# Where weights are decoded in the first slots of a fused top-k attention and feed-forward kernel

## The chip, the cores and the metric

The kernel runs on one core of a Trainium2 chip. The metric is the device time of one launch in microseconds. The engines are named as the profile names them: PE is TensorE's matmuls, PEld its weight loads, DVE is VectorE, ACT is ScalarE, POOL is GpSimd, and SP is the queue that issues most transfers.

## The reference

An attention that keeps, for each query, the 32 largest scores, and then a feed-forward that multiplies a hidden value by its own cosine.

```python
scores = scale * np.matmul(q, k.transpose(0, 1, 3, 2))      # 8 batches, 8 heads, 576 x 576, head size 64
kth = np.partition(scores, -top_k, axis=-1)[..., -top_k:-top_k + 1]
scores = np.where(scores >= kth, scores, -1000000000.0)
attn = np.exp(scores - np.max(scores, axis=-1, keepdims=True))
attn = attn / (np.sum(attn, axis=-1, keepdims=True) + 1e-09)
o = np.matmul(attn, v)
x = o.transpose(0, 2, 1, 3).reshape(4608, 512)
h = x @ w_in                                                  # 512 x 2048
out = (h * np.cos(h)) @ w_out                                 # 2048 x 512
```

q, k and v are single precision; w_in and w_out come in double precision, and the kernel turns them into single precision itself.

## The kernel before

**Units and slots.** The work is cut into 144 units: 36 blocks of 128 tokens by 4 pairs of heads. The main loop (L820) runs one slot for each unit. In slot i VectorE finds the 32 largest of each row of unit i, in four rounds of max and replace over two folded halves of the scores (`rest`, the larger of each pair, and `low`, the smaller). The same slot also ends the softmax of unit i-1 (`w`), sends the probabilities of unit i-2 (`x`) through memory to transpose them, and on even slots multiplies the probabilities of units i-4 and i-3 (`z`) with v. The scores of later units are made up to two slots ahead.

**Within a slot** (`slot`, L711) everything is issued by hand in one order, and each engine works through its own part of that order without overtaking. On VectorE: fold (L247), rounds 0 to 2 (L352 max, L357 replace), the shifts of the weights (L144), round 3 with the search of `low`, inside it the products that make xT (L486), then the sum and the reciprocal of the softmax (den L399, L404). On ScalarE: weight loads issued, sine (L592), mask (L381, L383), banks emptied (L551, L553, L622), exponentials (L391, with a table load after a sine), the copies of the next scores (L236, L237), and the first step of the weights' decoding (L133, L136). On GpSimd: the split of the probabilities into 16-bit halves (L424, L426), the making of `low` (L265, L274), the adds of the weights (L154), the reductions of the sine's argument (L573, L582), the gate g * cos (L599).

**`low` on two engines.** For units in `BUSY` (L95, 7 to 11) VectorE makes `low` itself with one more instruction (`fold_now`, L255). For the others GpSimd does it with an add and a subtraction (`fold_sum`, `fold_low`).

**Weights.** There are 32 chunks of 128 x 512, 16 of w_in and 16 of w_out. `load_weights` (L103) loads a number of them in each slot: in the first two slots on SP's queue, then on ScalarE's. A chunk is then decoded in three steps in a later slot: ScalarE (`decode_first`, at the end of the slot in which it was loaded), one shift on VectorE (`decode_second`) and one add on GpSimd (`decode_third`) in the next slot. `decode_third` takes the chunks last in, first out. Loaded chunks lie in seven buffers that the feed-forward's g also uses.

**Feed-forward.** `feed` (L646) is called three times in a slot and issues steps by credit: a step A b.i of the first product (`ff1`, block b, i from 0 to 7, 8 matmuls of 128 x 128) or a step B b.j of the second (`ff2`, two matmuls of 128 x 512). Two A steps fill one bank, which ScalarE empties (`take_banks`); after two banks GpSimd reduces the argument, ScalarE takes the sine, and GpSimd gates. `ff["kind"]` and `ff["half"]` hold which kind is next and whether one step of it has been done. A step is issued only when its weights have been decoded in an earlier slot and its gate lies two calls back; otherwise the other kind is taken. From the middle of the run a pair of slots holds 4 A steps, 4 B steps, the scores of 2 units and P@V of 2.

**P@V.** `values(z)` (L462 onwards, matmuls at L477) writes to a part of the bank `rim`, which also holds the ends of the scores. `take_values` (L481) makes xT of it, the input of the A steps: A b.0 needs xT of all four units of block b.

**Loads of the first slots.** `at_once` (L694 to L697) issues on SP's queue: v of head pair hp in slot hp, and q and k of pairs 2 and 3 in slots 0 and 1. Later loads have slots of their own (`at_slot`).

Of the kernel before, what the change touches and what calls it, by code (L numbers as in the profile page):

```python
# [30 lines left out]
def kernel(  # L31
# [16 lines left out]
    NP = H // 2  # L48
# [35 lines left out]
    for i in range(DF // CW):  # L84
        w = consts.tile([P, NC, CW], F32, tag=f"w_in{i}", name=f"w_in{i}")
# [4 lines left out]
    for f in range(NF):  # L90
        w = consts.tile([P, DM], F32, tag=f"w_out{f}", name=f"w_out{f}")
        w_out.append(w)
        chunks.append((moe_w_out[f * P : (f + 1) * P, :], w))
    CHUNKS, XB = 7, 4
    BUSY = range(7, 12)  # L95
    ff = {"live": 0, "tick": 0, "now": 0, "credit": 0.0, "end": False, "kind": 0, "half": 0, "open": 0, "late": False}

    wq = {"next": 0, "loaded": deque(), "second": deque(), "third": deque(), "done": 0, "ready": 0}
# [40 lines left out]
    def decode_second(n):  # L139

        for _ in range(min(n, len(wq["second"]))):
            st, w, spare = wq["second"].popleft()
            wi = w.bitcast(I32)
            nc.vector.tensor_scalar(  # L144
                out=wi, in0=wi, scalar1=3, scalar2=None, op0=ALU.logical_shift_left
            )
            wq["third"].append((st, w, spare))

    def decode_third():

        while wq["third"]:
            st, w, _ = wq["third"].pop()
            wi = w.bitcast(I32)
            nc.gpsimd.tensor_tensor(out=wi, in0=wi, in1=st[:, :, 0], op=ALU.add)  # L154
            wq["done"] += 1
# [5 lines left out]
    units = []  # L161
    for t0 in range(0, B * S, P):
        parts = []
        for i, a in enumerate((t0, t0 + TAIL)):
            b, q0 = a // S, a % S
# [75 lines left out]
    def fold_high(u):  # L241

        s, sc = u["s"], u["sc"]
        if u["n"] not in BUSY:
            del u["sc"]
# [5 lines left out]
    def fold_now(u):  # L251

        s, sc = u["s"], u.pop("sc")
        u["low"] = work.tile([P, 2, HS], F32, tag="low", name="low", bufs=1)
        nc.vector.tensor_tensor(  # L255
            out=u["low"], in0=sc[:, :, 0:HS], in1=s[:, :, HS:S], op=ALU.min
        )

    def fold_sum(u):

        if not u["folds"]:
            return
        s = u["s"].bitcast(I32)
        u["low"] = work.tile([P, 2, HS], F32, tag="low", name="low", bufs=1)
        nc.gpsimd.tensor_tensor(  # L265
            out=u["low"].bitcast(I32), in0=s[:, :, 0:HS], in1=s[:, :, HS:S], op=ALU.add
        )

    def fold_low(u):

        if not u["folds"] or u["n"] in BUSY:
            return
        low = u["low"].bitcast(I32)
        nc.gpsimd.tensor_tensor(  # L274
            out=low, in0=low, in1=u["rest"][:, :, HS:S].bitcast(I32), op=ALU.subtract
        )
# [15 lines left out]
    def topk_first(u, w):  # L292
# [5 lines left out]
        if u["folds"]:  # L298
            if u["n"] not in BUSY:
                fold_sum(u)  # L300
# [3 lines left out]
        if merges:  # L304
            merge_second(w)
        if u["folds"] and u["n"] in BUSY:
            fold_now(u)
        topk_round(u, 0, [lambda: bounds(w), lambda: distances(w)] if w else ())

    def topk_round(u, rnd, between=(), ahead=None):  # L310
        top, rest, lasts = u["top"], u["rest"], TOPK // 8 - 1
        end = TOPK - 1 - 8 * rnd
        at = top[:, :, end : end - 8 if rnd < lasts else None : -1, 0]
        if u["folds"]:
            search(
                at, rest[:, :, HS:S] if rnd == 0 else rest[:, :, 0:HS], rest[:, :, 0:HS], rnd < lasts,
                between if rnd < lasts else (),
            )
        else:
            search(at, u["s"] if rnd == 0 else rest, rest, rnd < lasts, between)  # L320
        if rnd < lasts:
            return
        del u["rest"]
        if u["folds"]:
            low = u.pop("low")
            for k in range(TOPK // 16):
                more = k < TOPK // 16 - 1
                if ahead and not more:
                    take_values(ahead)
                search(  # L330
                    top[:, :, 1 + 8 * k : 9 + 8 * k, 1], low, low, more,
                    () if more or rnd < lasts else between,
                )
# [10 lines left out]
    def merge_second(u):  # L344
        nc.vector.tensor_reduce(
            out=u["top"][:, :, TOPK - 1, 1], in_=u.pop("lesser"), axis=mybir.AxisListType.X,
            op=ALU.max,
        )

    def search(to, src, rest, more, between=()):  # L350
        for j in range(2):
            nc.vector.max(to[:, j], src[:, j])  # L352
            if between:
                between[j]()
        if more:
            for j in range(2):
                nc.vector.match_replace(rest[:, j], to[:, j], src[:, j], NEG)  # L357
# [39 lines left out]
    def sums(u):  # L397
        den = small.tile([P, 2], F32, tag="den", name="den")
        nc.vector.tensor_reduce(out=den, in_=u["den"], axis=mybir.AxisListType.X, op=ALU.add)  # L399
        u["den"] = den  # L400

    def reciprocal(u):
        u["rden"] = small.tile([P, 2], F32, tag="rden", name="rden")
        nc.vector.reciprocal(u["rden"], u.pop("den"))  # L404

    def both(u):
        return [lambda: sums(u), lambda: reciprocal(u)] if u else ()
# [71 lines left out]
    def take_values(us):  # L479
        blk, hp, n = block_of[us[0]["tok"]], us[0]["hp"], len(us)  # L480
        if "xT" not in blk:  # L481
            blk["xT"] = work.tile([P, NP, P], F32, tag="xT", name="xT", bufs=5)
        for i, u in enumerate(us):
            to, o, pT = blk["xT"][:, hp + i], room[0][:, i * P : (i + 1) * P], u.pop("pT")
            if u["paired"]:
                nc.vector.tensor_tensor(out=to, in0=o, in1=pT[:, 2 * NT + 1], op=ALU.mult)  # L486
            else:
                nc.scalar.copy(out=to, in_=o)
        blk["left"] -= n
        blk["tick"] = ff["tick"]  # L490
# [15 lines left out]
    first = deque((blk, i) for blk in blocks for i in range(2 * NF * blk["w"] // 512))  # L506
# [165 lines left out]
    LAST = NU - NP  # L672
# [7 lines left out]
    at_slot, at_once = {}, {}  # L680
# [7 lines left out]
    for n in range(NP, len(order)):  # L688
        i = last[order[n - 5]] if n >= 5 else 0
        load_at(max(i, 2 * NP + 2), load_qk, *order[n])  # L690
        i = last_values[order[n - 6]] if n >= 6 else 0
        load_at(max(i + 4 - i % 2, 2 * NP + 2), load_v, *order[n])

    for hp in range(NP):  # L694
        at_once[hp] = [(load_v, 0, hp)]
    for hp in range(2, NP):
        at_once[hp - 2].append((load_qk, 0, hp))  # L697

# [6 lines left out]
    def send(x):  # L705

        split(x)
        write_halves(x)
        transposes(x)

    def slot(i, u, w, x, z):  # L711
        n = (3, 4, 3, 2)[i] if i < NP else 2 if i < 2 * NP else 3
        if i < NP:
            for load, b, hp in at_once[i]:
                load(b, hp)
        load_weights(n, nc.sync if i < 2 else nc.scalar)
        if x:
            send(x)
        decoding = i < 3 * NP
        ff["late"] = False  # L720
        topk_first(u, w)
        fold_low(u)
        topk_round(u, 1)
        topk_round(u, 2)
        if decoding:
            sines(1)
            gate(1)
        decode_second(NP)
        decode_third()
        reduce_first()  # L730
        reduce_second()
        made = scored.get(i, [])
        if z:
            take_banks()
        feed(1)

        for m in made:
            scores(m)
        if z:
            values(z)  # L740


        late = len(made) > 0

        if i % 2 and not decoding:
            sines(1)
        if w:
            mask(w)
        take_banks()
        if w and late:  # L750
            exponentials(w)
        take_scores(units[i + 1])
        if w and not late:
            exponentials(w)
        topk_round(u, 3, both(w), z)
        ff["late"] = not decoding
        if i in at_slot:
            load, b, hp = at_slot[i]
            load(b, hp)
        gate(1)  # L760
        feed(1 if len(made) == 2 else 2)
        take_banks()
        decode_first(NP)
        reduce_first()
        reduce_second()
        feed(1 if len(made) == 2 else 3)
        if i == LAST:
            sines(1)
# [51 lines left out]
    for i in range(NU + 1):  # L820
        ff["end"] = i >= NU
        ff["credit"] = min(ff["credit"] + 5.0 - 0.9 * len(scored.get(i, [])), 5.3)
        ff["now"] += 1
        wq["ready"] = wq["done"]
        u, w = (units[i - n] if 0 <= i - n < NU else None for n in range(2))
        x = units[i - 2] if 0 <= i - 2 < LAST else None
        z = units[i - 4 : i - 2] if i % 2 == 0 and 0 <= i - 4 < LAST else None
        if i <= LAST:
            slot(i, u, w, x, z)
        else:  # L830
            last_slot(i, u, w, x, z)
# [47 lines left out]
```

## Time and profile before

| | |
|---|---|
| median of three runs (lowest, highest) | 1460.69 us (1459.52, 1464.77) |
| profiled execution: device time, span | 1461.65 us, 1459.9 us |
| busy share of the span: PE, PEld, DVE, ACT, POOL | 95%, 68%, 93%, 75%, 79% |
| span by the chain that ended last: PE, DVE, ACT, DMA | 82%, 8%, 4%, 3% |
| sum of A steps on PE (L537) and of B steps (L612) | 540.1 us, 538.1 us |
| sum of max (L352) and replace (L357) on DVE, four groups | 1221.3 us |
| the weights' decoding on POOL: the mean of one add (L154) | about 1.26 us |

Shares of busy time are means over the whole span. The page's picture of the span in 40 slices, each 36.5 us long, shows the start and the end apart:

```profile
PE   4387899999999999999999999999999999999998
DVE  7999999999999999999999999999999999999821
PEclk6598999999999999999999999999999999999999
DMA  8986687666665576657655666657665566655300
```

Each digit is the busy share of one slice in tenths. The first four slices or so are a start in which there is little feed-forward yet and the DMA engines are full; then PE and DVE are both full; in the last two slices the attention is done and only the feed-forward of the last blocks is left.

Slots can be found in the trace by L247, the first large instruction of a slot on DVE: slot 0 starts at 7.28 us, slot 1 at 17.83, slot 7 at 81.57, slot 8 at 91.86, slot 9 at 103.92, slot 10 at 114.55, slot 11 at 127.48, slot 12 at 138.11, slot 13 at 147.98, slot 14 at 158.81.

### The profile page before, as it was taken

What the parts mean: (1) busy time and instruction counts of PE and PEld (TensorE: products, weight loads), DVE (VectorE), ACT (ScalarE), POOL (GpSimd) and SP (SyncE); (2) the same over time, 40 slices, a digit from 0 to 9 for tenths busy, and PEclk for the clock granted to TensorE, in tenths of its full rate; (3) what the DMA queues carried; (4) which work ended last, traced back from release to release, by engine and by line L of the source; (5) the groups of instructions that cost most, each with busy time, mean ns of one, the idle gap of its engine ahead of it and who ended that gap; (6) DMA issues with size and microseconds to landing.
All of it is one profiled execution on the core that took longest, in us unless ns stands there. A gap on an engine that the chain in (4) does not pass through costs nothing.

```text
span 1459.9 us, 30230 instructions
## 1 busy us (share of the span) xinstructions
PE 1386.9 (95%) x10288; PEld 996.8 (68%) x10288; DVE 1363.8 (93%) x5213; ACT 1088.2 (75%) x1910; POOL 1157.5 (79%) x812
## 2 busy tenths in 40 slices
PE   4387899999999999999999999999999999999998
PEld 2265667777777767777777776777777777777665
DVE  7999999999999999999999999999999999999821
ACT  5787767877777777778777777777777787877641
POOL 5867878888888888888888887888888888888410
PEclk6598999999999999999999999999999999999999
DMA  8986687666665576657655666657665566655300
GB/s 254 282 235 192 175 183 182 155 161 190 179 159 152 168 180 169 161 144 201 185 168 143 144 180 182 170 149 185 192 169 144 152 171 168 166 152 152 62 8 15
DMA packets 427434, 240.00 MB, mean 164 GB/s; under 512 B 375952, under 2 KB 392592, under 8 KB 427280
## 3 DMA queue, kind: packets, MB, share of 16 engines
q1 hardware_dynamic: 418704, 216.88, 57.0%
q10 hardware_dynamic: 8576, 21.19, 4.1%
q8 instruction: 81, 1.33, 0.4%
q14 instruction: 73, 0.60, 0.1%
HBM read 45.09 MB, written 101.19 MB: 100 GB/s over the span
## 4 chain that ended last, share of the span: by engine, by line
PE 82%; DVE 8%; ACT 4%; DMA 3%; POOL 1%; issue 1%; SPq 1%; ACTq 0%; POOLq 0%
PE mm L537 31%; PE o L612 31%; PE rim L477 10%; PE sc L226 7%; DVE top L352 4%; DVE rest L357 2%; PE rim L226 2%; DMA v<-in_v_dram 1%; ACT s L391 1%; ACT s L383 1%; DMA k<-in_k_dram 1%; ACT L391 1%; DMA st<-in_moe_w_in_dram 1%; DVE rest L247 1%; DVE low L357 0%
## 5 line engine op out<-in xcount | busy, mean ns | idle before, releaser
L537 PEld LDWEIGHTS mm<-xT,w_in 128*128 128x128 f32 x4608 | 537.0, 192 | 74.8 <-issue 64.7
L612 PE MATMUL o<-w_out,g 128*128 128x512 f32 x1152 | 538.1, 600 | 12.0 <-POOL w_out L154 7.7
L537 PE MATMUL mm<-xT,w_in 128*128 128x128 f32 x4608 | 540.1, 275 | 6.8 <-ACT x L553 3.9
L352 DVE MAX8 top<-rest 128x8 f32<-128x288 f32 x1148 | 480.7, 454 | 0.0
L424 POOL COPY halves<-s 128x2304 uint16<-128x2304 uint16 x140 | 294.8, 2105 | 149.5 <-ACT s L391 149.1
L357 DVE MATCH_REPLACE8 rest<-top,rest 128x288 f32<-128x288 f32 (+1 forms) x860 | 377.0, 446 | 0.0
L612 PEld LDWEIGHTS o<-w_out,g 128*128 128x128 f32 x1152 | 202.4, 190 | 199.0 <-issue 184.2
L352 DVE MAX8 top<-low 128x8 f32<-128x288 f32 x568 | 240.0, 448 | 0.1
L391 ACT ACTIVATE s<-s,nd 128x576 f32<-128x576 f32 x288 | 220.2, 767 | 0.8
L383 ACT ACTIVATE s<-s,top 128x576 f32<-128x576 f32 x288 | 206.1, 766 | 0.0
L274 POOL TENSOR_TENSOR low<-low,rest 128x576 int32<-128x576 int32 x137 | 193.6, 1413 | 10.7
L265 POOL TENSOR_TENSOR low<-s 128x576 int32<-128x576 int32 x137 | 193.7, 1414 | 6.1 <-ACT s L237 4.9
L226 PE MATMUL sc<-k,q 64*128 64x448 f32 (+1 forms) x640 | 157.9, 591 | 36.8 <-DMA k<-in_k_dram 14.9
L551 ACT ACTIVATE g<-mm 128x512 f32<-128x512 f32 x144 | 85.8, 596 | 128.8 <-PE mm L537 124.6
L582 POOL TENSOR_TENSOR x<-g,x 128x1024 f32<-128x1024 f32 x68 | 160.9, 2366 | 5.7
L477 PE MATMUL rim<-pT,v 128*64 128x128 f32 (+1 forms) x2560 | 159.5, 269 | 2.8 <-DMA pT<-rows 2.8
L599 POOL TENSOR_TENSOR g<-g,x 128x1024 f32<-128x1024 f32 x68 | 161.0, 2367 | 1.3 <-ACT x L592 1.3
L477 PEld LDWEIGHTS rim<-pT,v 128*64 128x64 f32 x2560 | 132.8, 139 | 13.1 <-issue 4.0
L236 ACT COPY s<-sc 128x896 f32<-128x896 f32 x144 | 129.2, 897 | 3.9 <-PE sc L226 3.4
L237 ACT COPY s<-rim 128x256 f32<-128x256 f32 x144 | 55.1, 382 | 91.9 <-PE rim L477 91.9
L357 DVE MATCH_REPLACE8 low<-top,low 128x288 f32<-128x288 f32 x284 | 123.6, 443 | 0.0
L226 PEld LDWEIGHTS sc<-k,q 64*128 64x128 f32 (+1 forms) x640 | 47.5, 183 | 100.2 <-DVE rest L357 47.0
(59 smaller groups left out, 1335.8 us busy)
## 6 DMA issues: line engine op xcount, KB each, us to landing
rows<-halves SPq DMA_DIRECT2D x140, 640.0 KB, 3.0
out_dram<-ob ACTq DMA_DIRECT2D x36, 256.0 KB, 2.4
q<-in_q_dram SPq DMA_DIRECT2D x31, 288.0 KB, 3.9
v<-in_v_dram SPq DMA_DIRECT2D x32, 256.0 KB, 3.4
st<-in_moe_w_out_dram ACTq DMA_DIRECT2D x16, 512.0 KB, 5.1
st<-in_moe_w_in_dram SPq DMA_DIRECT2D x10, 512.0 KB, 6.9
k<-in_k_dram SPq DMA_DIRECT2D x31, 144.0 KB, 3.8
k<-in_k_dram SPq DMA_DIRECT2D x32, 128.0 KB, 3.8
```

What stands on the lines that cost most here:

```text
L226: nc.tensor.matmul(to[r0 : r0 + rows, j, 0 : k1 - k0], st["q"][d, q0 : q0 + rows], st["k"][d, k0:k1], start=True, stop=True,)
L265: nc.gpsimd.tensor_tensor(out=u["low"].bitcast(I32), in0=s[:, :, 0:HS], in1=s[:, :, HS:S], op=ALU.add)
L274: nc.gpsimd.tensor_tensor(out=low, in0=low, in1=u["rest"][:, :, HS:S].bitcast(I32), op=ALU.subtract)
L352: nc.vector.max(to[:, j], src[:, j])
L357: nc.vector.match_replace(rest[:, j], to[:, j], src[:, j], NEG)
L383: nc.scalar.activation(out=s[:, j], in_=s[:, j], func=AF.Prelu, bias=less[:, j, 1:2], scale=1.0, alpha=FAR)
L391: nc.scalar.activation(out=s[:, j], in_=s[:, j], func=AF.Exp, bias=nd[:, j : j + 1], scale=SCALE, accum_out=den[:, j, 0:1],)
L424: nc.gpsimd.tensor_copy(out=halves[:, :, 0 : 2 * S], in_=s.rearrange("p (k h) -> p h k", h=2))
L477: nc.tensor.matmul(o[d, to], lhsT, rhs, start=c == 0, stop=c == NT)
L537: nc.tensor.matmul(mm[:, at : at + w], w_in[f // FC][:, c, (f % FC) * P : (f % FC + 1) * P], blk["xT"][:, c], start=c == 0, stop=c == NC - 1,)
L599: eng.tensor_tensor(out=g, in0=g, in1=x, op=ALU.mult)
L612: nc.tensor.matmul(o, g[:, at : at + P], w_out[f], start=f == 0, stop=f == NF - 1)
```

## The change

There are six edits.

- `BUSY` begins at unit 8: `low` of unit 7 is made on GpSimd.
- The numbers of chunks loaded in each slot are 3, 3, 3, 2, 2, 2, 3, 3, 3, 3, then 2, instead of 3, 4, 3, 2, 2, 2, 2, 2, then 3.
- From slot 7 on (`early` false) the shifts and adds of the weights stand after round 3 instead of after round 2, and the adds take the chunks first in, first out.
- v of pair 3 is loaded in slot 2, together with v of pair 2, instead of in slot 3.
- P@V of units 0 and 1 is made in slot 5 instead of slot 4; units 2 and 3 follow in slot 6 as before.
- On even slots from 12 on, the kind of the next feed-forward step is set: the second half of an open bank of A if there is one, else B.

```diff
-    BUSY = range(7, 12)
+    BUSY = range(8, 12)
...
-    def decode_third():
+    def decode_third(early):
 
         while wq["third"]:
-            st, w, _ = wq["third"].pop()
+            st, w, _ = wq["third"].pop() if early else wq["third"].popleft()
...
     for hp in range(NP):
-        at_once[hp] = [(load_v, 0, hp)]
+        at_once.setdefault(min(hp, 2), []).append((load_v, 0, hp))
...
     def slot(i, u, w, x, z):
-        n = (3, 4, 3, 2)[i] if i < NP else 2 if i < 2 * NP else 3
+        n = (3, 3, 3, 2, 2, 2, 3, 3, 3, 3)[i] if i < 10 else 2
+        early = i < 2 * NP - 1
+        if i % 2 == 0 and i >= 3 * NP:
+            ff["kind"], ff["half"] = (0, 1) if first and first[0][1] % 2 else (1, 0)
         if i < NP:
-            for load, b, hp in at_once[i]:
+            for load, b, hp in at_once.get(i, ()):
                 load(b, hp)
...
-        decode_second(NP)
-        decode_third()
+        if early:
+            decode_second(NP)
+            decode_third(early)
         reduce_first()
         reduce_second()
...
         topk_round(u, 3, both(w), z)
+        if not early:
+            decode_second(NP)
+            decode_third(early)
         ff["late"] = not decoding
...
-        z = units[i - 4 : i - 2] if i % 2 == 0 and 0 <= i - 4 < LAST else None
+        z = units[i - 4 : i - 2] if i % 2 == 0 and NP < i < LAST + 4 else None
+        if i == NP + 1:
+            z = units[0:2]
```

The order in which instructions are issued changes up to slot 12 and is the same from slot 13 to the end. In slots 7 to 12 the changed kernel has shifts of 3, 3, 2, 3, 2 and 1 chunks, where the kernel before has 2, 2, 3, 2, 3 and 1. The adds of slots 7, 9 and 11 stand ahead of the reductions and of the next slot's split on GpSimd. In slot 12 the step A 1.5 is issued ahead of the scores, where it stood after P@V.

## The prediction

> **What bounds the kernel now.** I read the table of windows first, one row per stretch, with each engine's busy time, the granted TensorE clock and the DMA share.
>
> ```profile
> 25.00:50.00 25.00, 7.93 (x24) 3.54 (x24) 23.42 (x87) 21.57 (x43) 21.66 (x18) 0.50 0.96 282
> 100.00:125.00 25.00, 17.34 (x91) 9.80 (x90) 24.93 (x84) 20.84 (x39) 18.07 (x13) 0.80 0.67 211
> 150.00:175.00 25.00, 21.57 (x155) 14.86 (x154) 23.36 (x91) 20.22 (x35) 22.81 (x16) 1.00 0.56 167
> 300.00:400.00 100.00, 100.00 (x720) 72.73 (x719) 98.93 (x388) 78.86 (x136) 86.99 (x61) 1.00 0.68 184
> 1350.00:1400.00 50.00, 45.95 (x354) 33.67 (x353) 39.49 (x115) 33.34 (x65) 22.96 (x19) 1.00 0.23 47
> ```
>
> From 175 to 1350 us TensorE (first column after the length) has no gap worth naming. Before 150 us it idles and VectorE (third) is full. So there are two regimes, and I looked for the seam in the timeline of TensorE:
>
> ```profile
> 115.26 2.08 PE L612 MATMUL o<-w_out,g 128*128 128x512 f32 x2 [7.66 <-POOL w_out L154]
> ...
> 156.83 1.98 PE L612 MATMUL o<-w_out,g 128*128 128x512 f32 x4 [2.16 <-POOL g L599]
> ...
> 167.08 3.39 PE L537 MATMUL mm<-xT,w_in 128*128 128x128 f32 x28 [1.27 <-DVE xT L486]
> ```
>
> The last gap ends at 167.08, where the first feed-forward matmul of block 2 waits for VectorE's xT of slot 14 (issued at 166.75). Everything after is TensorE work in a fixed order, 1292.8 us to the end of the span. The orders of issue of the two kernels agree on every engine from slot 13 on, and by the end of slot 12 both have issued the same feed-forward work. So the end moves by what slot 14's xT moves, and only slots 1 to 13 count.
>
> In those slots VectorE is the clock. Its timeline (start, length, operation, idle before) shows the stalls, two of them inside the shift's own duration:
>
> ```profile
> 61.85 0.75 DVE L247 TENSOR_TENSOR rest<-sc,s 128x576 f32<-128x576 f32 x1
> 71.51 0.75 DVE L247 TENSOR_TENSOR rest<-sc,s 128x576 f32<-128x576 f32 x1
> 81.57 0.75 DVE L247 TENSOR_TENSOR rest<-sc,s 128x576 f32<-128x576 f32 x1
> 87.85 0.75 DVE L144 TENSOR_SCALAR w_out<-w_out 128x512 int32<-128x512 int32 x2
> 98.14 1.97 DVE L144 TENSOR_SCALAR w_out<-w_out 128x512 int32<-128x512 int32 x2
> 120.83 3.00 DVE L144 TENSOR_SCALAR w_out<-w_out 128x512 int32<-128x512 int32 x2
> 158.11 0.16 DVE L399 TENSOR_REDUCE den<-dens 128x2 f32<-128x4 f32 x1 [1.56 <-ACT s L391]
> ```
>
> Two shifts cost 0.75 us alone but 1.97 and 3.00 here. GpSimd's timeline says why, and also shows the chain from the adds to the gate in slots 7 and 8:
>
> ```profile
> 88.73 2.57 POOL L154 TENSOR_TENSOR w_out<-w_out,st 128x512 int32<-128x512 int32 x2 [5.75 <-ACT s L391]
> 91.26 1.07 POOL L573 TENSOR_SCALAR x<-x 128x1024 f32<-128x1024 int32 x1
> 92.41 2.36 POOL L582 TENSOR_TENSOR x<-g,x 128x1024 f32<-128x1024 f32 x1
> 94.72 2.10 POOL L424 COPY halves<-s 128x2304 uint16<-128x2304 uint16 x1
> 97.12 2.37 POOL L599 TENSOR_TENSOR g<-g,x 128x1024 f32<-128x1024 f32 x1
> ...
> 121.01 2.53 POOL L599 TENSOR_TENSOR g<-g,x 128x1024 f32<-128x1024 f32 x1
> ```
>
> Both long shifts end just after a gate multiply (L599). The add's 5.75 us wait is put down to ScalarE, which had long been done; it begins 0.13 us after the shift, so the shift is what it waited for.
>
> **What the Trainium skill says.** "SBUF — State Buffer", Who interferes with whom: VectorE and GpSimd share a port pair as an exclusive lock; tensor_scalar can take it, and whoever comes second is blocked for the other's whole instruction. The trace agrees: at 120.83 one of the two shifts took 2.58 us. "TensorE: Matmul & The Clock Gate", What's actually happening: after an idle window of about 3.4 us the array runs at half rate until it has been busy about as long. The trace agrees: after the 7.66 us gap the two halves of a w_out product took 2.08 us, against 1.88 for four halves at 139.51.
>
> **The change part by part.** A slot runs from one L247 to the next. Slot 5 is 9.66 us with two shifts (0.66 net), so a bare slot is 9.0; the two xT products add 0.40, a fold on VectorE (L255) 0.63 net, each shift 0.34.
>
> *Slots 1 to 6 (fewer early chunks, P@V of units 0 and 1 in slot 5, last v one slot sooner).* Before, 17.83 to 81.57 is 63.74 us. After: six bare slots 54.0, 15 shifts (3, 3, 3, 2, 2, 2) 5.1, two xT pairs 0.8, so 59.9. To this I add 0.3 that the same sum leaves unexplained before. Kept: the waits of 0.27 before L247 of units 2 and 3, and about 0.5 for slot 4's shift behind fold_low on GpSimd (before 0.62). Gone: 0.79 at den in slot 2 (one decode of 1.13 us less on ScalarE ahead of the exponentials), 0.25 at slot 2's fourth shift, 0.80 at xT in slot 4. That makes 61.2; slot 7 starts near 79.1, 2.5 earlier. Bounds 1 (the queue's transfers, at a DMA share of 0.96 here, eat it: v moves in front of the first probabilities' 640 KB on SP's queue) and 3.8 (no stall at all). P@V costs nothing in slot 5: the same 6.6 us of TensorE, idle there; its xT pair moves with it.
>
> *Unit 7's fold to GpSimd.* VectorE saves 0.63. GpSimd gets 1.41 + 1.42 us right after the split, where it idled 5.75; hidden.
>
> *Shifts and adds at the end, slots 7 to 12.* Fourteen shifts instead of 13, +0.34. The collisions (1.28, 2.24 and 0.24 in slots 8, 10, 12) and 1.83 in slot 13 lose their cause. TensorE's 7.66 us gap goes too, since chunk 23 is added in slot 8 instead of 9, first come first served; that alone brings nothing, as VectorE had no idle time there.
>
> What comes late instead: the sine of the feed-forward. In slot 7 the adds now follow round 3, and the two reductions (L573, L582) stand behind them, then the split, then the gate. Counted from slot 7's start: first shift 8.86, three adds of 1.26 and 3.4 for the reductions end near 16.5 (before: 13.2). The sine in slot 8 waits for that, and ScalarE has a bank, mask, a table load and the exponentials queued behind it: 94.80 to 101.38 before, 6.58. Exponentials end at 23.1; VectorE asks for den at 10.03 + 9.36 = 19.4. **A new stall of 3.7 us.** The same in slot 10: 1.5. In slot 12 the split waits behind slot 11's two adds, so fold_low ends about 1.1 after low is searched, and the single shift meets L582 (0.5).
>
> *First in, first out.* Before, the adds took the last shift's weights first, so GpSimd started after all shifts. Now the first add may start after one. With three shifts it asks at about 0.42 + 0.13 = 0.55 us, the third shift at 0.67, and an add holds it 1.26. Bounds: 0 to 1.3 in each of slots 7, 8 and 10; I take half, 0.65, since the trace shows such a slip once (120.83), behind another operation. It delays the adds some 0.3 as well.
>
> Sum, from slot 7's start: slot 8 at 10.7; den of slot 8 at 23.4 (stall 3.4), slot 9 at 25.8; slot 10 at 36.1; den at 47.4 (stall 1.9), slot 11 at 49.8; slot 12 at 60.1; stalls 1.4 and 0.5, slot 13 at 71.7; slot 14 at 80.8 and its xT 7.9 later. That is 79.1 + 88.7 = 167.8 against 166.75: **+1.05 us**. The early slots' 2.5 are given back.
>
> *Order of the feed-forward.* It only sets A1.5 ahead of the scores in slot 12, so its bank is emptied before ScalarE's sine of slot 13; that removes the 1.56 us at den, counted above.
>
> The span becomes 1461.0. The profiled execution took 1461.65 in all and its span was 1459.9; the runs' median is 1460.69, so I forecast 1461.7.
>
> **The rivals.**
> *Hidden after all (faster).* If the sine's chain isn't late, slots 7 to 13 take 71.5 us instead of 77.24, and with the early 2.5 slot 14 comes 8.2 sooner: 1452.5. For it: VectorE had no other waits than those named. Against: the 3.4 us of the reductions behind three adds is plain arithmetic.
> *The lock (slower).* If every shift but the first waits for an add, slots with three lose 2.5 and slots with two 1.26: 10.0 in five slots. Slot 7's share disappears in the stall that follows, 7.5 remain, and GpSimd's chain is later by about another 1 in slots 8 and 10: +8 to +9, 1469. It decides once an add gets in before the second shift. Against: the second shift asks 0.33 after the first, before the semaphore can have reached GpSimd.
> *The early gain missing.* DMA traffic holds slot 7 where it was: 1464.2. For it, the DMA share of 0.96; against, a chunk of 512 KB less is in the way.
>
> **How the numbers follow.** Forecast with its neighbours (the third rival included, within 0.5%, 7.3 us, about what a measurement here can tell from no change) 0.70; faster 0.15; slower 0.15. The range of the forecast alone is 1457 (no slip, 3.8 early) to 1466 (full slip +2.5, and slot 14's values on a cold array, 0 to 4, after a 4 us gap before them). Reaching to the other cases: 1453 to 1469.
>
> **What would show it.** Right: slot 7's L247 near 79, shifts after the reciprocal, a wait of den for ScalarE in slot 8 of 2 to 4 us, no gap before w_out, slot 14's xT within 3 us of 166.75, no TensorE gap after. Wrong: slot 8's den without a wait (then faster); shifts of 2 us or more in slots 7 to 11 (then slower); TensorE gaps after 170 us, which would break the tie between slot 14 and the end.

## The result, and the profile after

| | before | changed |
|---|---|---|
| median (lowest, highest), five runs each | 1459.52 us (1458.85, 1464.77) | 1468.73 us (1466.35, 1471.63) |
| ratio of the times, 95% interval | | 1.0056 (1.0032 to 1.0080) |
| profiled execution: device time, span | 1461.65, 1459.9 us | 1468.73, 1466.9 us |

The changed kernel is slower by 0.56%. (This ratio, like those below, is taken over all runs and is not the quotient of the two medians.) The table of windows, for three of the stretches shown of before (length, then busy time of PE, PEld, DVE, ACT, POOL, then granted clock, DMA share, GB/s):

```profile
100.00:125.00 25.00, 17.79 (x82) 10.58 (x84) 19.02 (x67) 17.99 (x33) 14.96 (x12) 0.77 0.72 211
150.00:175.00 25.00, 20.37 (x165) 13.10 (x162) 23.16 (x87) 17.09 (x32) 24.24 (x19) 0.86 0.58 167
300.00:400.00 100.00, 100.00 (x733) 72.28 (x734) 98.77 (x387) 78.18 (x140) 86.81 (x60) 1.00 0.63 176
```

From 175 us on TensorE is full as before. Between 100 and 125 us VectorE, which had been busy 24.93 us of 25, is busy 19.02: a new stall of about six microseconds lies there. TensorE's timeline at the seam:

```profile
130.24 3.39 PE L612 MATMUL o<-w_out,g 128*128 128x512 f32 x4 [2.97 <-POOL g L599]
...
166.16 3.78 PE L612 MATMUL o<-w_out,g 128*128 128x512 f32 x4 [4.63 <-POOL g L599]
...
176.70 3.73 PE L537 MATMUL mm<-xT,w_in 128*128 128x128 f32 x32
```

The 7.66 us gap before a product with w_out is gone. But the last gap is now the one that ends at 166.16, where a product with w_out waits for GpSimd's gate; it took 1.98 us at this place before and takes 3.78 now. The first product of block 2, whose wait ended the last gap before, follows at 176.70 with no idle time. Its matmuls end at 180.43 (176.70 + 3.73) instead of 170.47 (167.08 + 3.39), ten microseconds later. The end of the span is 7.0 us later. Three microseconds come back on the way: product by product, TensorE is 9.96 us behind before at 180 us, 8.80 from 203 us on, 7.48 from 542 and 7.0 to 7.2 from 882 on. The second step lies where before waited for a late k (0.17 us at 539.48, with slow matmuls around it), the third where each of the two waited for one (0.17 us at 878.91, 0.22 at 886.43). The first step has no wait beside it, and its cause stays open.

VectorE's timeline shows where the ten microseconds come from:

```profile
57.55 0.75 DVE L247 TENSOR_TENSOR rest<-sc,s 128x576 f32<-128x576 f32 x1
...
81.30 0.75 DVE L247 TENSOR_TENSOR rest<-sc,s 128x576 f32<-128x576 f32 x1
...
90.09 1.08 DVE L144 TENSOR_SCALAR w_out<-w_out 128x512 int32<-128x512 int32 x3
91.22 0.75 DVE L247 TENSOR_TENSOR rest<-sc,s 128x576 f32<-128x576 f32 x1
...
105.98 0.49 DVE L486 TENSOR_TENSOR xT<-rim,pT 128x128 f32<-128x128 f32 x2 [6.10 <-ACT s L237]
106.76 0.14 DVE L399 TENSOR_REDUCE den<-dens 128x2 f32<-128x4 f32 x1
107.24 2.17 DVE L144 TENSOR_SCALAR w_out<-w_out 128x512 int32<-128x512 int32 x3
109.47 0.74 DVE L247 TENSOR_TENSOR rest<-sc,s 128x576 f32<-128x576 f32 x1
...
132.12 0.49 DVE L486 TENSOR_TENSOR xT<-rim,pT 128x128 f32<-128x128 f32 x2 [3.79 <-ACT s L237]
133.38 2.17 DVE L144 TENSOR_SCALAR w_out<-w_out 128x512 int32<-128x512 int32 x3
135.61 0.74 DVE L247 TENSOR_TENSOR rest<-sc,s 128x576 f32<-128x576 f32 x1
```

Slot 5 starts at 57.55, 4.30 us ahead of before. Slot 7 starts at 81.30, only 0.27 ahead. Slot 8 then takes 18.25 us (from 91.22 to 109.47) instead of 12.06, with a wait of 6.10 us at xT. Slot 10 takes 15.92 instead of 12.93, with a wait of 3.79. The three shifts at the end of slots 8 and 10 take 2.17 us, and 1.08 in slot 7.

The two waits are longer than what they cost. From the start of slot 7 to that of slot 11 the changed kernel takes 54.31 us, before 45.91: 8.40 more. Of these, 3.78 are a later xT in slot 8 (24.68 us after slot 7's start instead of 20.90) and 0.52 a later xT in slot 10 (22.65 after slot 9's start instead of 22.13). The other 2.04 and 2.06 lie between xT and the next slot, where the shifts now stand. The rest of each wait is mostly time that before spent on shifts in the middle of the slot. So the loss has two parts of about the same size: ScalarE's copy comes later, and the shifts come behind xT.

Both waits are for ScalarE's copy of the scores' last columns (L237). ScalarE's timeline in slot 8:

```profile
94.05 1.28 ACT L592 ACT_TABLE_LOAD   x1 [1.22 <-POOL w_out L154]
...
98.32 1.15 ACT L592 ACTIVATE x<-x,halfpi 128x1024 f32<-128x1024 f32 x1 [2.99 <-POOL x L582]
...
101.97 1.28 ACT L391 ACT_TABLE_LOAD   x1
103.26 0.77 ACT L391 ACTIVATE s<-s,nd 128x576 f32<-128x576 f32 x1
...
104.04 0.76 ACT L391 ACTIVATE s<-s,nd 128x576 f32<-128x576 f32 x1
...
104.80 0.88 ACT L236 COPY s<-sc 128x896 f32<-128x896 f32 x1
105.58 0.37 ACT L237 COPY s<-rim 128x256 f32<-128x256 f32 x1
```

The sine (L592) waits for GpSimd, and everything below stands behind it in ScalarE's order. Ahead of it stand the table load and the loads of weights, and these have waited 1.22 us for the adds already. The copy ends at 105.95 and xT starts at 105.98. GpSimd's timeline shows the front of the chain, and also what ate the early gain:

```profile
61.36 2.10 POOL L424 COPY halves<-s 128x2304 uint16<-128x2304 uint16 x1 [4.38 <-DMA rows<-halves]
...
90.64 4.20 POOL L154 TENSOR_TENSOR w_out<-w_out,st 128x512 int32<-128x512 int32 x3 [5.13 <-DVE w_out L144]
94.81 1.04 POOL L573 TENSOR_SCALAR x<-x 128x1024 f32<-128x1024 int32 x1
95.93 2.35 POOL L582 TENSOR_TENSOR x<-g,x 128x1024 f32<-128x1024 f32 x1
```

The adds that waited for the end of slot 7 (90.64) hold the reductions back until 98.28; L582 ended near 94.77 before. Earlier, in slot 5, the split waits 4.38 us until a transfer of probability rows has read its buffer; fold_low comes late behind it, and VectorE waits for `low` (3.8 us in three waits in the first 185 us, where the profile of before lists none).

Before was already at the edge of this wait. ScalarE's timeline and then VectorE's, of the kernel before, in its slot 8:

```profile
102.06 0.37 ACT L237 COPY s<-rim 128x256 f32<-128x256 f32 x1
```

```profile
102.47 0.49 DVE L486 TENSOR_TENSOR xT<-rim,pT 128x128 f32<-128x128 f32 x2
```

The copy ended at 102.43 and xT began at 102.47 with no idle time shown: the two engines arrived together. Any delay of ScalarE there goes straight into VectorE's time. And what VectorE does before xT, such as a shift in the middle of the slot, is paid only beyond the moment at which that copy is done.

### The profile page after: what moved, and what is told of

The parts are those of the page before. It is cut to its first block, busy times and chain, and to the rows that moved or that the text cites. A ratio compares the mean times of both kernels' runs of the same rounds, so it can differ in the third digit from the quotient of the medians.

```text
span 1466.9 us, 30248 instructions
## 1 busy us (share of the span) xinstructions
PE 1389.5 (95%) x10288; PEld 1000.3 (68%) x10288; DVE 1361.7 (93%) x5212; ACT 1088.2 (74%) x1910; POOL 1162.1 (79%) x814
## 4 chain that ended last, share of the span: by engine, by line
PE 83%; DVE 8%; ACT 3%; DMA 2%; POOL 2%; SPq 1%; issue 1%; ACTq 0%; POOLq 0%
PE o L612 32%; PE mm L537 31%; PE rim L477 10%; PE sc L226 7%; DVE top L352 3%; PE rim L226 2%; DVE rest L357 2%; DMA rows<-halves 1%; ACT s L391 1%; DVE rest L247 1%; ACT s L383 1%; ACT L391 1%; DVE low L357 0%; DMA st<-in_moe_w_in_dram 0%; POOL w_out L154 0%
## 5 line engine op out<-in xcount | busy, mean ns | idle before, releaser
L226 PE MATMUL sc<-k,q 64*128 64x448 f32 (+1 forms) x640 | 154.1, 588 | 32.5 <-DMA k<-in_k_dram 13.9
L477 PE MATMUL rim<-pT,v 128*64 128x128 f32 (+1 forms) x2560 | 161.4, 271 | 8.9 <-DMA pT<-rows 6.1
L582 POOL TENSOR_TENSOR x<-g,x 128x1024 f32<-128x1024 f32 x68 | 160.9, 2367 | 5.7
L477 PEld LDWEIGHTS rim<-pT,v 128*64 128x64 f32 x2560 | 134.1, 140 | 19.5 <-DMA pT<-rows 4.4
L237 ACT COPY s<-rim 128x256 f32<-128x256 f32 x144 | 55.1, 382 | 91.4 <-PE rim L477 91.4
L247 DVE TENSOR_TENSOR rest<-sc,s 128x576 f32<-128x576 f32 x142 | 106.1, 747 | 6.3 <-ACT s L237 6.3
```

Source lines behind the costliest of these rows:

```text
L226: nc.tensor.matmul(to[r0 : r0 + rows, j, 0 : k1 - k0], st["q"][d, q0 : q0 + rows], st["k"][d, k0:k1], start=True, stop=True,)
L477: nc.tensor.matmul(o[d, to], lhsT, rhs, start=c == 0, stop=c == NT)
L582: nc.gpsimd.tensor_tensor(out=x, in0=g, in1=x, op=ALU.subtract)
```

## The experiments

Each had five rounds beside the kernel before on the same chip, 9 to 22 executions in all. The "time" is the median; "late" and "middle" say whether a slot's shifts and adds stand behind round 3 or behind round 2 of the search. No run leaves out any part of the computation.

| run | what it is | time | before | ratio (95%) |
|---|---|---|---|---|
| mid_slot | early edits, all middle | 1460.00 | 1461.48 | 0.9994 (0.9971 to 1.0017) |
| late_only | before, late from slot 7 | 1468.56 | 1461.48 | 1.0042 (1.0031 to 1.0053) |
| lifo | changed, late adds in the old order | 1470.06 | 1461.48 | 1.0056 (1.0044 to 1.0069) |
| reduce_first | changed, reductions ahead of late adds | 1466.32 | 1461.48 | 1.0030 (1.0018 to 1.0041) |
| odd_late | changed, late in 7, 9, 11 alone | 1466.47 | 1459.70 | 1.0048 (1.0031 to 1.0064) |
| even_late | changed, late in 8, 10, 12 alone | 1463.83 | 1459.70 | 1.0029 (1.0019 to 1.0040) |
| before_even | before, late in 8, 10, 12 alone | 1459.67 | 1459.70 | 1.0001 (0.9990 to 1.0013) |
| even_lifo | even_late, adds in the old order | 1463.83 | 1460.25 | 1.0023 (1.0011 to 1.0035) |
| mid_fewer | mid_slot, fewer chunks in slots 4, 5 | 1457.16 | 1460.25 | 0.9992 (0.9970 to 1.0015) |
| before_kick | before, feed-forward's order edit alone | 1458.58 | 1460.25 | 0.9993 (0.9977 to 1.0008) |
| mid_fewest | mid_slot, one chunk in slots 3 to 5 | 1458.76 | 1462.27 | 0.9973 (0.9962 to 0.9985) |
| late_fewer | changed, fewer chunks in slots 4, 5 | 1470.44 | 1462.27 | 1.0054 (1.0031 to 1.0076) |

**The two halves of the change.** mid_slot keeps all early edits and leaves the shifts where they were:

```diff
-        early = i < 2 * NP - 1
+        early = True
```

> All edits of the change kept but one: in every slot the shifts and adds stand after round 2, last in first out, as before. Theory sine (adds ahead of the reductions make the sine late, and xT of slots 8 and 10 waits for ScalarE's copy behind the exponentials): the waits of 6.1 and 3.8 us go, slot 14's xT comes at 166 to 169 instead of 175.4, and the time falls to 1459 to 1462. Theory start (the early edits, P@V in slot 5 and the transfers, cost the time): stays at 1466 to 1469.

late_only does the reverse: before, with the calls of the shifts and adds put behind round 3 from slot 7 on and their order first in, first out.

> The kernel before with one edit: from slot 7 on the shifts and adds stand after round 3, first in first out. Its slots 7, 9 and 11 decode 2, 3 and 3 chunks. Theory sine: a wait of some 4 us at xT of slot 8 and of 4 to 5 at that of slot 10 appears, 1466 to 1470. Theory start: 1459 to 1461, as before.

mid_slot can't be told from before; late_only has most of the loss. VectorE's timelines, mid_slot first, then late_only:

```profile
101.97 3.37 DVE L144 TENSOR_SCALAR w_out<-w_out 128x512 int32<-128x512 int32 x3
107.56 0.47 DVE L486 TENSOR_TENSOR xT<-rim,pT 128x128 f32<-128x128 f32 x2
```

```profile
103.25 0.49 DVE L486 TENSOR_TENSOR xT<-rim,pT 128x128 f32<-128x128 f32 x2 [4.86 <-ACT s L237]
...
129.53 0.49 DVE L486 TENSOR_TENSOR xT<-rim,pT 128x128 f32<-128x128 f32 x2 [5.03 <-ACT s L237]
```

In mid_slot three shifts take 3.37 us in slot 8, because GpSimd's gate multiply runs from 102.20 to 104.73, and yet xT comes just when ScalarE's copy ends (107.51): this slip costs little. In late_only, xT waits about five microseconds in slots 8 and 10. So the late place is the cause of the loss. The early edits alone cost nothing that can be told from no change, and they don't cure it.

**The order of the adds.** lifo takes the late adds in the old order, last chunk first, so that they can't start between two shifts:

```diff
-            st, w, _ = wq["third"].pop() if early else wq["third"].popleft()
+            st, w, _ = wq["third"].pop()
```

> The changed kernel, with the late adds taken last in first out again, so that the first add waits for the last shift. Theory lock (first in first out lets an add in between shifts): the shifts of slots 8 and 10 go from 2.17 to 1.1 us, and the time falls by 1 to 2 us, to 1466 to 1468. Theory sine: the rest of the loss stays; xT still waits 6 us in slot 8.

VectorE's timeline, slot 8 of lifo:

```profile
105.78 0.49 DVE L486 TENSOR_TENSOR xT<-rim,pT 128x128 f32<-128x128 f32 x2 [6.38 <-ACT s L237]
...
107.05 1.08 DVE L144 TENSOR_SCALAR w_out<-w_out 128x512 int32<-128x512 int32 x3
```

The three shifts fall from 2.17 to 1.08 us, as they must if an add held the third one, and the time does not fall (1.0056 both times). The slip is real and is no part of the loss that can be measured: the waits at xT stay. In the trace about half of what the shifts save is given back, because the adds start later and the sine with them (17.30 us after slot 7's start instead of 17.02, and 16.87 after slot 9's instead of 16.05): from slot 7 to slot 11 lifo takes 53.20 us, the changed kernel 54.31. A gain of one microsecond lies within the intervals.

**What the sine waits for.** reduce_first moves the late adds alone behind the two reductions of the feed-forward:

```diff
         if not early:
             decode_second(NP)
-            decode_third(early)
         ...
+        if not early:
+            decode_third(early)
```

> The changed kernel, with the late adds moved behind the two reductions on GpSimd; the shifts stay after round 3. Theory sine: the reductions of slot 7 start 4 us sooner and those of slot 9 2.6, so the waits at xT in slots 8 and 10 fall to 2 and 1 us, and the time to 1461 to 1464. If the shifts' place itself costs the time, 1466 to 1469.

VectorE's timeline, slots 7 and 8 of reduce_first:

```profile
88.95 4.58 DVE L144 TENSOR_SCALAR w_out<-w_out 128x512 int32<-128x512 int32 x3
...
104.02 0.49 DVE L486 TENSOR_TENSOR xT<-rim,pT 128x128 f32<-128x128 f32 x2 [1.79 <-ACT s L237]
```

In slot 10 the move does what it was meant to do: the wait at xT falls from 3.79 to 0.75 us, and xT comes 19.61 us after slot 9's start instead of 22.65. So there the adds ahead of the reductions are what delays ScalarE. In slot 8 the wait falls from 6.10 to 1.79 us for another reason. The shifts, still behind round 3, now meet the reductions on the shared port and take 4.58 us instead of 1.08, so slot 8 itself begins 3.50 later after slot 7's start. (The Trainium skill, "SBUF — State Buffer", Who interferes with whom, says that the second comer is blocked for the other's whole instruction; L573 runs here from 88.25 and L582 from 89.39 to 91.83, the first add follows at 91.78, and of the three shifts one takes 2.60 us and one 1.50; they end at 93.53.) Counted from slot 7's start, xT of slot 8 comes at 23.86 us, hardly sooner than the 24.68 of the changed kernel. ScalarE's timeline shows why:

```profile
95.07 1.28 ACT L592 ACT_TABLE_LOAD   x1 [3.44 <-POOL w_out L154]
96.36 1.15 ACT L592 ACTIVATE x<-x,halfpi 128x1024 f32<-128x1024 f32 x1
```

The sine no longer waits for a reduction. But ScalarE issues the loads of weights ahead of it, and a load needs a buffer that an add frees, so ScalarE waits 3.44 us for the adds themselves. Late adds thus hold the sine on two paths: through the reductions queued behind them, and through the buffers. With one path gone in slot 8 the other takes its place, and no run removes both while the adds stay late. The waits at xT came out as the first theory said, the time (1466.32) as the second: about half of the loss goes.

**Which slots.** odd_late and even_late split the late place between slots 7, 9, 11 and slots 8, 10, 12:

```diff
-        early = i < 2 * NP - 1
+        early = i < 2 * NP - 1 or i % 2 == 0
```

> The changed kernel with the late place kept in slots 7, 9 and 11 only, whose adds stand ahead of the reductions or of slot 12's split; in 8, 10 and 12 shifts and adds stand after round 2 again. Theory sine: nearly the whole loss stays, xT waits 4 to 6 us in slots 8 and 10, 1466 to 1469. Rival lock (the shifts' new places collide with GpSimd in 8 and 10): 1460 to 1463.

even_late has `i % 2 == 1` in that place.

> The changed kernel with the late place kept in slots 8, 10 and 12 only. Theory sine: no loss stays, and the shifts of slots 8 and 10 no longer meet the gate's multiply, so xT of slots 8 and 10 waits under 2 us, and the time is 1457 to 1460, 1 to 3 below the kernel with every shift after round 2. Rival lock: 1465 to 1468.

before_even is before with the same parity and the old order of the adds.

> The kernel before with one edit: in slots 8, 10 and 12 the shifts and adds stand after round 3, last in first out. Theory sine: the shifts of 1.97 and 3.00 us become 0.75 each, nothing gets late, and the time falls 2 to 4 us below before, 1456 to 1458. If the early edits bring anything, it is slower than even_late; if not, the two are alike.

odd_late alone has most of the loss (1.0048). Counted from slot 7's start, xT of slot 8 comes at 24.67 us in odd_late, as in the changed kernel (24.68), and at 21.83 in even_late, as in mid_slot (21.87): the place of slot 7's adds sets it. That the even slots would be a gain was wrong, and wrong twice: even_late is slower than before by 0.29%, and before_even equals before where 2 to 4 us of gain were expected. VectorE's timeline, slot 8, odd_late first, then even_late:

```profile
97.87 3.84 DVE L144 TENSOR_SCALAR w_out<-w_out 128x512 int32<-128x512 int32 x3
...
106.34 0.49 DVE L486 TENSOR_TENSOR xT<-rim,pT 128x128 f32<-128x128 f32 x2 [2.34 <-ACT s L237]
```

```profile
103.00 0.49 DVE L486 TENSOR_TENSOR xT<-rim,pT 128x128 f32<-128x128 f32 x2 [3.19 <-ACT s L237]
...
104.26 2.17 DVE L144 TENSOR_SCALAR w_out<-w_out 128x512 int32<-128x512 int32 x3
```

In odd_late the shifts of slot 8 collide (3.84 us) and xT still has 2.34 us to wait: even that collision is under cover. In even_late VectorE waits 3.19 us with nothing to do, where mid_slot had its 3.37 us of shifts, and shifts afterwards, 2.17 us on the path. A middle place in the even slots uses a wait that is there anyway; the late place pays for the shifts.

before_even has only two shifts there, of 0.74 us together. It stands 4.2 us below even_late on the same chip. The early edits (three shifts in slots 8 and 10, not two) and the order of the adds separate the two; why that makes 4.2 us is not shown. before_even's profile is of its longest run (1466.57 us) and says nothing of its median, but it shows something else. ScalarE's timeline in its slot 8:

```profile
106.59 0.37 ACT L237 COPY s<-rim 128x256 f32<-128x256 f32 x1 [4.69 <-PE rim L477]
```

Here the sine is on time (13.23 us after slot 7's start, as before), and yet xT waits 6.72 us: the copy waits for P@V (L477), which had waited 8.18 us for the transposed probabilities to arrive. So the copy can be late by a transfer too, in some executions.

even_lifo asks whether the slip of the shifts is what remains in even_late: the adds are taken in the old order everywhere.

> The changed kernel with the late place in slots 8, 10 and 12 alone, and the late adds carried out last chunk first, so that no add follows at GpSimd while the next shift runs. Theory that the lock lengthens the end of these slots: the three shifts behind xT fall from 2.17 us to about 1.1 in slots 8 and 10, and the time from 1463.8 to 1461 to 1462.5 (1.0015 of the kernel before). Theory that the slip of the shifts is covered by the wait for GpSimd's next split, or is only moved into another wait: the shifts are 1.1 us, and the time stays at 1463 to 1465.

VectorE's timeline, slot 8 of even_lifo:

```profile
105.47 0.49 DVE L486 TENSOR_TENSOR xT<-rim,pT 128x128 f32<-128x128 f32 x2 [4.25 <-ACT s L237]
...
106.73 1.07 DVE L144 TENSOR_SCALAR w_out<-w_out 128x512 int32<-128x512 int32 x3
```

The shifts halve again and the median is the same, 1463.83. The time lies where the second theory put it, though the ratio's interval takes in the first theory's 1.0015 too: the slip is worth nothing that these runs can tell. (The waits of the two profiles can't be compared here: in even_lifo's slot 8 the copy waits 0.96 us for P@V and its transfer.)

**What ties the last slots to the end.** before_kick takes from the change only the line that sets the order of the feed-forward from slot 12 on:

```diff
+        if i % 2 == 0 and i >= 3 * NP:
+            ff["kind"], ff["half"] = (0, 1) if first and first[0][1] % 2 else (1, 0)
```

> The kernel before with one edit of the change alone: from slot 12 on, P@V parts with both halves are issued in even slots, so that the kick of slot 13 does not wait. Theory that the last slots are tied at xT of slot 14: the wait of 1.6 us at den in slot 13 goes, and the time falls by 1 to 1.5 us (0.9990 to 0.9993). Theory that they are tied at the gate for the first B product of unit 1 in slot 14: the wait at den goes, B1.0 starts within 0.5 us of 156.8, and the time stays within 0.5 us.

VectorE's timeline, then ScalarE's and TensorE's:

```profile
165.21 0.49 DVE L486 TENSOR_TENSOR xT<-rim,pT 128x128 f32<-128x128 f32 x2 [0.86 <-ACT s L237]
```

```profile
164.81 0.37 ACT L237 COPY s<-rim 128x256 f32<-128x256 f32 x1 [2.78 <-PE rim L477]
```

```profile
155.56 3.78 PE L612 MATMUL o<-w_out,g 128*128 128x512 f32 x4 [3.67 <-POOL g L599]
...
166.51 3.73 PE L537 MATMUL mm<-xT,w_in 128*128 128x128 f32 x32
```

xT of slot 14 is 1.54 us sooner than before (166.75), but that is not the edit's work: slot 12, where the edit begins to act, starts at 136.86 instead of 138.11, so this execution was 1.25 us ahead already. Counted from slot 12's start, xT is 0.29 us sooner and the product at 155.56 comes at 18.70 us, where it came at 18.72 before (156.83). The wait at den in slot 13 does fall, from 1.56 to 0.37 us. What it gave is lost in slot 14: xT waits for ScalarE's copy, the copy for P@V, and P@V stands on TensorE behind the product that waited for the gate and then ran on a slow array, 3.78 us against 1.98. Block 2's matmuls end at 170.24 against 170.47. The ratio's interval takes in both theories; the trace speaks for the gate. Before, the gate's chain and xT stood within 1.3 us of each other (the 1.27 us for which block 2 waited).

**The early gain.** mid_fewer is mid_slot with one chunk of weights instead of two asked for in slots 4 and 5, and one more in each slot from 10 on:

```diff
-        n = (3, 3, 3, 2, 2, 2, 3, 3, 3, 3)[i] if i < 10 else 2
+        n = (3, 3, 3, 2, 1, 1, 3, 3, 3, 3)[i] if i < 10 else 3
```

> All early edits of the change, with every unit's shifts and adds left in the middle of the slot, and the weight rows asked for in slots 4 and 5 cut to two and one chunks of three, one more in each of the later slots. Theory that the rows queued behind the pT transposes in slots 4 and 5 give the early gain back: the wait of GpSimd's split for its rows in slot 5 falls from 4.4 us to under 2, slot 7 starts by 80, and the time is 1457 to 1459 where the same kernel with three chunks in each had 1460. Theory that the number of rows asked for is not the cause: that wait stays near 4 us, slot 7 starts at 81 or later, and the time stays at 1460.

(Its "two and one chunks of three" is this line: slot 3 keeps two chunks, slots 4 and 5 have one each, and mid_slot had two in each of the three.)

mid_fewest has `(3, 3, 3, 1, 1, 1, 3, 3, 3, 3)` there, and late_fewer is the changed kernel with mid_fewer's line.

> All early edits, every unit's shifts and adds in the middle of the slot, and one chunk of weights asked for in each of slots 3, 4 and 5 (the run with two, one and one had 1457.2 us, that with two in each 1460.0). Theory that fewer weight rows in the queues make the rows of the split arrive sooner: its wait in slots 5 and 6 together stays under 3.4 us, slot 7 starts by 78, and the time is 1455 to 1458. Theory that the earlier run's gain was the luck of one execution, or that the chunks left out are missed later: slot 7 starts after 79 or TensorE waits over 4 us for weights in slots 8 to 10, and the time is 1460 or more.

> The changed kernel whole, late place from slot 7 on included, with two, one and one chunks of weights asked for in slots 3, 4 and 5. Theory that early gain and late loss are separate and add: slot 7 starts at 78 to 79, scores' copies hold up xT by 4 to 6 us in slots 8 and 10 as before, and the time is 1464.5 to 1467, 2 to 4 below the changed kernel. Theory that the late loss swallows what is won early, because the waits there end on a transfer that comes at its own time: slot 7 starts by 79 and the time stays at 1468 or above.

GpSimd's timelines, the split of slots 5 and 6, of mid_fewer and then of mid_fewest:

```profile
59.12 2.10 POOL L424 COPY halves<-s 128x2304 uint16<-128x2304 uint16 x1 [1.36 <-DMA rows<-halves]
68.14 2.10 POOL L424 COPY halves<-s 128x2304 uint16<-128x2304 uint16 x1 [2.02 <-DMA rows<-halves]
```

```profile
57.83 2.10 POOL L424 COPY halves<-s 128x2304 uint16<-128x2304 uint16 x1 [2.99 <-DMA rows<-halves]
70.06 2.10 POOL L424 COPY halves<-s 128x2304 uint16<-128x2304 uint16 x1 [5.22 <-DMA rows<-halves]
```

mid_fewer did in the profiled execution what the first theory wanted: slot 7 at 78.08, span 1452.8 us. But its runs reach from 1452.77 to 1471.11, and the ratio shows no gain. mid_fewest is faster than before by 0.27%, the only version here that is; yet in its profile the split waits 8.2 us and slot 7 starts at 79.29. That the fewer chunks are what helps is not shown, since the interval of mid_slot, which has two chunks in those slots, overlaps with mid_fewest's (0.9971 to 1.0017, and 0.9962 to 0.9985); nor is the reason given for it, a shorter wait of the split. What the gain comes from stays open.

late_fewer didn't repeat it (1.0054). Up to slot 7 it has the same instructions as mid_fewer, and yet its slot 7 starts at 85.32. Its profiled execution, the longest of its runs, has xT waits of 6.13 and 3.80 us, as the changed kernel had, and two waits of TensorE for decoded w_out of 7.84 and 6.38 us. Fewer chunks early together with late adds leave the products without weights, so this run doesn't say whether the early gain and the late loss add.

## Why the prediction was right or wrong

The time lay in the range, 0.3 us below its upper end, but above the forecast by 7 us. The largest chance, 0.70, went to a change within 0.5%; measured are 0.56% (0.32 to 0.80). That the range held is luck. The forecast's own range ended at 1466, and 1469 stood there for the rival of the lock, in which every shift but the first waits for an add, 10 us in five slots; of these 10 us 2.18 came, and they are not seen in the time.

In the sum, xT of slot 14 was to come at 167.8 us and came at 175.40. Of these 7.6 us, 2.2 were there at slot 7's start, 4.5 came in slots 7 to 10 (54.31 us where 49.8 were forecast) and 1.0 in slot 14 (8.93 for 7.9). Slots 11 to 13 were right: 30.86 us, and 31.0 forecast.

*The seam* was taken a step too far. "The end moves by what slot 14's xT moves" failed: xT came 8.65 us later (175.40 against 166.75) and block 2's matmuls ended 9.96 later. The B step that waits for the gate was the true tie in the changed kernel: it came 9.33 us later (166.16 against 156.83) and lost another 1.8 us on the slow array. xT itself hung on it, waiting 0.91 us for a copy that waited 2.78 us for P@V behind that product. The range had this as a case ("0 to 4, after a 4 us gap"); the forecast had it at nothing.

*Slots 1 to 6*: slot 7 was to start at 79.1 and started at 81.30. The third rival, the early gain missing, came true, and not in one execution alone. In the seven profiles with these early edits (changed, lifo, reduce_first, odd_late, even_late, even_lifo, mid_slot) slot 7 starts at 80.16 to 85.69; in the four without them (before, late_only, before_even, before_kick), at 79.52 to 81.57. The sum held up to slot 5; the term that was left out is GpSimd's split, which waits until the rows' transfer has read its buffer, and then fold_low behind it. In slots 5 and 6 together this wait is 5.5 to 6.8 us in those seven profiles and 0 to 1.2 in the four.

*Unit 7's fold to GpSimd* was hidden, as said: slot 7 took 9.92 us, with no wait for `low` in it.

*Late shifts and adds.* The chain was right, but for the path through the buffers, and its waiter wrong. The reductions were to end 16.5 us after slot 7's start and ended at 16.98; the exponentials at 23.1, measured 23.50. But the stall was put at den, to be 3.4 in slot 8 and 1.9 in slot 10. The trace of before showed that xT, which stands 0.8 us ahead of den on VectorE, starts right after ScalarE's copy (L237), and ScalarE makes its two copies after the exponentials, 1.15 us more. So VectorE stops earlier and is released later: 6.10 and 3.79 us, 4.6 more in sum. For the same reason two of the signs pointed the wrong way: den of slot 8 had no wait, which was to mean a faster kernel, and the shifts of 2.17 us, which were to mean the lock, came without its cost. Slot 12's part was right: a wait of 1.20 us for `low`, and a slot of 11.42 us where 11.6 were forecast.

*First in, first out*: the slip was half of one add in three slots by forecast (1.95 in sum), and was 1.09 in slots 8 and 10 and none in slot 7 (2.18). The sum was near, and its worth was not seen: lifo and even_lifo take it away and the time stays.

*The collisions lose their cause*, counted as a gain in slots 8 and 10, was the second wrong term. Before's slips of 1.28 and 2.24 us lay ahead of xT, and xT could not have started before ScalarE's copy was done: at 102.43 in slot 8, where it started at 102.47, and at 125.27 in slot 10, where it started at 126.05. So at most 0.04 and 0.78 us were to be had, not 3.5, and the shifts behind xT cost 0.74 each in return. before_even measures the sum: nothing. *The kick*: the 1.56 us at den were counted as a gain; in before_kick 1.19 of them go, and 0.29 reach xT of slot 14. That xT comes 1.54 us sooner there, so near to 1.56, is chance.

*The 7.66 us gap* of TensorE went and brought nothing, as said.

## What to carry to other kernels

Before taking a slip on one engine as a loss, look at the next instruction of that engine that depends on another: if it starts the moment the other engine is done, the slip was under cover, and moving work from before that instruction to behind it makes it dearer, not cheaper. When a delay runs through an engine's queue, follow it to the first waiter in the other engine's order and to the last instruction queued before the release, here a copy behind the exponentials, not the exponentials. A wait is not its cost: what counts is how much later the waiting instruction starts, from a point that the change doesn't move. The last gap of a start-up can have a neighbour a microsecond behind it, as here; cost both. And before two profiles are compared at a late point, compare them where the edit begins to act.

## What the runs showed of the hardware

A product of four w_out halves took mostly 1.88 to 1.98 us on a busy array. It took 3.78 after idle times of 2.46 us (lifo, at 129.75), 3.21 (mid_slot), 3.67 (before_kick) and 4.63 (changed), but 3.52 after 3.90 (even_lifo) and 2.62 after 3.89 (even_late). The Trainium skill gives an idle window of about 3.4 us, which runs freely ("TensorE: Matmul & The Clock Gate", What's actually happening); 2.46 us were enough here. The length of the last gap alone doesn't set the price either. The last two cases have nearly the same gap behind the same products, and differ in when the granted clock falls: in even_late it is 1.00 for the first 1.17 us of the product (159.33 to 160.50) and 0.51 in the 1.5 us after that; in even_lifo it has fallen by 160.7, before the product starts at 161.02. Where a gap lies in a freely running window would explain that, but no run here tests it.

Three shifts in a row on VectorE took 1.07 to 1.09 us where no add could start before the last of them (lifo, even_lifo), and 2.17 in slots 8 and 10 of the changed kernel, where the first add started 0.49 us after the first shift: one add gets in once, ahead of the third shift, not between each two. In slot 7 the first add started 0.55 us after the first shift (90.64 and 90.09), and nothing slipped (1.08 us). What decides between the two is not shown.
